# Keys loaded in runs of four positions of a head, and transposed as identity products of single heads on the two column halves

## The chip, the cores and the metric

The kernel runs on one core of one Trainium2 chip. The metric is the device time of one execution in microseconds (us); the time of a kernel is the median of several runs. One further execution is taken with the hardware profiler, and all durations below come from it. PE is the matrix engine (PEld its weight loads), DVE, ACT and POOL are the vector, scalar and GpSimd engines, SP is the engine whose queue issues most DMAs.

## The reference

Attention with a mix of the heads before and after the softmax, then a feed-forward layer with the gate `h - tanh(h)`:

```python
scores = scale * np.matmul(q, k.transpose(0, 1, 3, 2))      # q, k, v: (8, 12, 448, 64)
scores = np.einsum('bhij,hg->bgij', scores, w_pre)          # over the 12 heads
scores = scores - np.max(scores, axis=-1, keepdims=True)
attn = np.exp(scores)
attn = attn / (np.sum(attn, axis=-1, keepdims=True) + 1e-09)
attn = np.einsum('bhij,hg->bgij', attn, w_post)
attn_out = np.matmul(attn, v)
x = attn_out.transpose(0, 2, 1, 3).reshape(3584, 768)
h = x @ w_in                                                # (768, 2048)
out = (h - np.tanh(h)) @ w_out                              # (2048, 768)
```

All data are float32.

## The kernel before, in words

The first half of the program is the attention. Each of the 8 batches is cut into four blocks of at most 120 query positions. For a block the kernel transposes the queries (`prep_q`), multiplies them with the transposed keys (`scores`, tiles `ps_q`, copied to `s`), and lets DMAs regroup the scores so that all 12 heads of 10 positions lie in one tile (`gather`, t<-s, two per place). Then come the mix of the heads (`premix`, tile `ps_p`), the maximum and the exponential (`expo`), the weights of the second mix with the sums of the softmax in them (`norm`, tile `wr`, on POOL), the second mix, which also transposes (`mix`, tile `ps_o`), and the product with the values (`values`, tile `ps_m`, operands `at` and `vr`).

The work is laid out in *places*: one pass of the loop `for p in range(NPL + 3)` (line 1256) handles two groups of 10 positions. A table `todo`, worked out ahead of the loop, says at which place a block's `scores`, `values`, `prep_q`, `prep_k` and loads stand. The order on each engine is the order in which the code is written, and is kept by hand (`in_order`). DMAs on SP are issued in order at the places; the weights of the feed-forward layer are split into parts by `Convert` at the same time (tiles `cr`, `co`, `ct`), with its own loads and stores on the SP queue. The second half of the program is the feed-forward layer.

The keys come in by 24 loads, three for each batch: `load_k(b, hq)` loads four heads. Position `4p + c` of a head goes to partition p (112 partitions, four positions c each). Before, the tile `kr` is laid out as [c, head, d]; a run that is contiguous in memory on both sides is one position of one head, 64 numbers or 256 bytes. `prep_k(b, hp)` then transposes a pair of heads: for each c, the 112x128 numbers of the two heads are one transpose on PE (line 814), which fills 112 columns of a PSUM tile, one head on partitions 0 to 63 and the other on 64 to 127. ACT copies the result as the high part (`kh`, line 825) and DVE subtracts to get the low part (`kl`, line 826). Two `prep_k` calls stand at one place, so the transposes come in groups of eight; there are 24 such groups, of which three belong to the start, ahead of the loop. The values are loaded (`load_v`) as [head, c, d], in runs of four positions or 1 KB.

Of the kernel before, what the change touches and what calls it, by code (L numbers as in the profile page):

```python
# [10 lines left out]
F32 = mybir.dt.float32  # L11
# [10 lines left out]
def raw(ap):  # L22

    return ap.bitcast(F32)
# [126 lines left out]
def kernel_body(  # L151
# [11 lines left out]
    nc = tc.nc  # L163
    B, H, S, D = q.shape
# [4 lines left out]
    CP = 112  # L169
    NC = S // CP  # L170
# [565 lines left out]
    with ExitStack() as st:  # L736

        early, early_ps = ctx.enter_context(ExitStack()), ctx.enter_context(ExitStack())
        ld = early.enter_context(tc.tile_pool(name="ld", bufs=2, side="left"))
# [4 lines left out]
        kp = st.enter_context(tc.tile_pool(name="kp", bufs=1, side="right"))  # L744
# [5 lines left out]
        ident = cst.tile([P, P], F32, name="ident")  # L750
# [3 lines left out]
        kks, vts, krs, qrs, qbs, sts, ats = {}, {}, {}, {}, {}, {}, {}  # L754


        queue, slow, sent = [], [], {}

        def dma(dst, src, to=None):
            entry = [place[0], dst, src, None]  # L760
            (queue if to is None else to).append(entry)
            return lambda places=0: entry[3] is not None and entry[3] + places <= place[0]
# [13 lines left out]

        def load_k(b, hq, t=None):
            if t is None:
                t = ld.tile([CP, NC, 4, D], F32, name="kr", tag="kr", bufs=2)

            sent[b, hq, "k"] = dma(t, k[b, 4 * hq : 4 * hq + 4].rearrange("h (p c) d -> p c h d", c=NC))
            krs[b, hq] = t

        def load_v(b, hq):
# [19 lines left out]
        halves = (slice(0, D), slice(D, P))  # L804

        def prep_k(b, hp, ps=None):


            hq, r = hp // 2, hp % 2
            assert sent[b, hq, "k"]()  # L810
            if ps is None:
                ps = ps_m.tile([P, 512], F32, name="ps_m", tag="ps_m")
            for c in range(NC):
                nc.tensor.transpose(
                    ps[:, c * CP : (c + 1) * CP],
                    krs[b, hq][:, c, 2 * r : 2 * r + 2].rearrange("p j d -> p (j d)"),
                    ident[:CP, :CP],
                )

            def rest():  # L820
                if r == 0:
                    kk = ld.tile([P, 2, 2, S], F32R, name="kk", tag="kk", bufs=KB)
                    kks[b, hq] = kk[:, 0], kk[:, 1]
                kh, kl = kks[b, hq]
                nc.scalar.copy(kh[:, r], ps[:, :S])  # L825
                then.append(lambda: nc.vector.tensor_sub(kl[:, r], ps[:, :S], raw(kh[:, r])))
                if r == 1:
                    del krs[b, hq]

            sooner.append(rest)  # L830
# [79 lines left out]
        def premix(p):  # L910


            pss = [ps_p.tile([P, S], F32, name="ps_p", tag="ps_p") for _ in halves]
            ts = [tg.pop(2 * p + j) for j in range(2)]
            for j in (1, 0):
                for r in (1, 0):
                    k = slice(r * D, D + r * H * half_rows(2 * p + j)[r])
                    nc.tensor.matmul(pss[r][halves[j], :], wpre[k, :], ts[j][k, :], start=True, stop=True)  # L918
            return pss
# [112 lines left out]
        def now(*engines):  # L1032
            place[0] += 1
            engines = engines or (nc.sync,)
            for x in (queue, slow):
                while x:
                    send(x, engines[len(x) % len(engines)])
# [2 lines left out]
        load_q(0)  # L1040
        now()
        for hq in range(3):
            load_k(0, hq, kp.tile([CP, NC, 4, D], F32, name="tmp_k", tag="x", bufs=1) if hq == 2 else None)
        now()
        load_q(1, kp.tile([MT, H, D], F32, name="tmp_q", tag="at", bufs=2))
        now()
# [34 lines left out]
        for w in range(2):  # L1081
            for at in AT[w]:
                x = repeat[:, w, at : at + HP].rearrange("p (i h) -> p i h", i=GH)
# [7 lines left out]
        for w in range(2):  # L1091
            for a in range(2):
                if w == 0:
                    x = both[:, w, a].rearrange("p (i g) -> p i g", i=GH)
                    of, step = ps_w[:, w, :].unsqueeze(1).to_broadcast([P, GH, H]), [[H, GH], [0, H]]
                else:
                    x = both[:, w, a].rearrange("p (g i) -> p g i", i=GH)
# [18 lines left out]
        for r in range(2):  # L1116
            prep_k(0, r, ps_k[:, r])
        flush()
        busy(4, ps_m.tile([P, 512], F32, name="ps_b", tag="ps_m"))
        prep_k(0, 2, bank())  # L1120
        prep_k(0, 3, bank())
        scores_of(0, 0)
        flush()
# [41 lines left out]
        at_s, p, kind = {}, 0, None  # L1165
        window = {i: (lo, hi) for lo, hi, k, i, _ in sorted(halved, reverse=True) if k == "s"}
        while halved:
            ready = sorted((x for x in halved if x[0] <= p), key=lambda x: (x[1], x[3:]))
            if ready:
                x = ready[0]  # L1170
# [3 lines left out]
                if x[2] == kind and other and x[1] > p + 1:  # L1174
                    x = other[0]
# [25 lines left out]
        for i, (b, m) in enumerate(blocks):  # L1201
            p0 = first[i] // 2
            if i + 2 < len(blocks):
                p = at_s[i + 2, 0] - 1
# [7 lines left out]
        for b in range(1, B):  # L1212
            p, o, done = first[blocks.index((b - 1, 1))] // 2 - 4, 0, []
            for hq in range(3):
                if hq == 2:

                    p = max(p, done[0] + 1)
                at_place(p, load_k, b, hq)
                o = max(p + 4, o + 1)
                p += 1  # L1220
                if hq > KB - 4:

                    o = max(o, end_s[blocks.index((b - 1, 3)), hq - 1 - (KB - 4)] + 1)
                for r in range(2):

                    while any(f is prep_q for f, *a in todo[o]) or 2 * len(held(o)) + sum(f is values for f, *a in todo[o]) > 2:
                        o += 1
                    at_place(o, prep_k, b, 2 * hq + r)
                done.append(o)
                assert o < at_s[blocks.index((b, 0)), hq], (b, hq)  # L1230
# [7 lines left out]
        def between0(f):  # L1238
# [10 lines left out]
        start = {  # L1249
            NPL - 3: [partial(load_w0, 0)] + [partial(load_x0, c) for c in range(NK)],  # L1250
            NPL - 2: x0[:1],
            NPL - 1: [partial(load_w0, 1)],
            NPL + 1: [block0.step],
        }
        mixed = None
        for p in range(NPL + 3):
# [13 lines left out]
            if p < NPL:  # L1270
                ps = premix(p)
# [123 lines left out]
```

## Time and profile before

| | |
|---|---|
| time, median of 3 runs | 1708.94 us (1706.41 to 1719.01) |
| the profiled execution's own time | 1703.0 us |
| its span, first to last instruction | 1701.3 us |
| PE busy | 1660.1 us, 98% of the span, 16068 matmul records |
| DVE, ACT, POOL busy | 72%, 64%, 34% |
| mean granted TensorE clock | 0.994 |
| DMA packets under 512 bytes | 105264 of 322290 |

Busy time of PE is counted from a matmul's start to its modelled end, and matmuls overlap; what a matmul costs is therefore read from the distance of one start to the next, not from its duration. Attention and feed-forward layer have different limits, so the rows are read by stage: the places of the attention lie between about 30 and 840 us. Idle time of an engine is put down to what ended it.

### The profile page before, as it was taken

The numbers are of one execution on the slowest core, as the hardware profiler recorded it, in microseconds if no ns is written. First come the engines' busy times: TensorE is split into PE (matmuls) and PEld (weight loads), VectorE is DVE, ScalarE is ACT, GpSimd is POOL, SyncE is SP. The second block draws the span as 40 slices with busy tenths as digits, with TensorE's granted clock in tenths as the row PEclk, the third lists the DMA queues.
The fourth block names the chain that finished last, engine by engine and source line by source line (L and its number), as shares of the span: only waits on it lengthen the run. The fifth ranks groups of instructions, "written<-read, shape, count | busy, mean of one in ns | idle before, by whom it ended". The sixth has DMA issues, their size and how long they took to land.

```text
span 1701.3 us, 41215 instructions
## 1 busy us (share of the span) xinstructions
PE 1660.1 (98%) x16068; PEld 1379.8 (81%) x16068; DVE 1231.3 (72%) x2119; ACT 1091.1 (64%) x1920; POOL 585.5 (34%) x798
## 2 busy tenths in 40 slices
PE   8999999999999899999999999999999999999999
PEld 6777777777777677677788888888888888989999
DVE  5777777878777777675497899868778867778432
ACT  5777777777777677676586777556667456666331
POOL 1466667666666666662100111101001101011100
PEclk9999999999999999999999999999999999999999
DMA  8879889898987979856589899989999989988993
GB/s 183 218 228 257 255 246 276 247 270 259 256 253 231 269 234 257 254 182 208 190 269 340 273 331 318 346 295 335 318 334 362 368 272 327 326 311 327 404 413 132
DMA packets 322290, 475.09 MB, mean 279 GB/s; under 512 B 105264, under 2 KB 255280, under 8 KB 322096
## 3 DMA queue, kind: packets, MB, share of 16 engines
q1 hardware_dynamic: 305660, 414.34, 75.5%
q0 software_dynamic: 16128, 57.68, 8.7%
q8 instruction: 128, 2.10, 0.5%
q14 instruction: 66, 0.54, 0.1%
q10 hardware_dynamic: 308, 0.43, 0.1%
HBM read 274.73 MB, written 120.59 MB: 232 GB/s over the span
## 4 chain that ended last, share of the span: by engine, by line
PE 72%; DMA 7%; DVE 7%; ACT 4%; issue 4%; POOL 4%; SPq 1%; POOLq 0%; ACTq 0%; DVEq 0%
PE ps_o L957 11%; PE ps_h L291 8%; PE ps_h L292 7%; PE ps_h L294 7%; PE ps_m L999 6%; PE ps_p L918 6%; PE y L534 6%; PE y L532 6%; PE y L533 6%; PE ps_q L874 4%; DMA t<-s 2%; DMA gl<-gs 2%; ACT e L929 1%; DVE mx L927 1%; PE y L504 1%
## 5 line engine op out<-in xcount | busy, mean ns | idle before, releaser
L957 PEld LDWEIGHTS ps_o<-wr,e 60*112 60x112 f32 (+1 forms) x5760 | 303.3, 175 | 46.1 <-POOL wr L940 31.9
L957 PE MATMUL ps_o<-wr,e 60*112 60x60 f32 (+1 forms) x5760 | 314.5, 259 | 16.1 <-POOL wr L940 14.6
L929 ACT ACTIVATE e<-ps_p,mx 128x448 f32<-128x448 f32 x360 | 224.8, 631 | 117.2 <-DVE mx L927 82.8
L927 DVE TENSOR_REDUCE mx<-ps_p 128x1 f32<-128x448 f32 x360 | 206.5, 615 | 109.1 <-PE ps_p L918 108.5
L967 ACT COPY at<-ps_o 112x960 f32<-112x960 f32 x156 | 154.3, 989 | 103.4 <-PE ps_o L957 102.9
L918 PE MATMUL ps_p<-t,wpre 60*64 60x448 f32 (+1 forms) x1440 | 182.4, 570 | 6.7 <-DMA t<-s 6.6
L999 PEld LDWEIGHTS ps_m<-at,vr 112*64 112x64 f32 x3072 | 147.6, 137 | 23.0 <-issue 7.7
L999 PE MATMUL ps_m<-at,vr 112*64 112x120 f32 (+1 forms) x3072 | 161.4, 262 | 1.1 <-DMA vr<-in_v_dram 0.9
L532 PE MATMUL y<-w,gh 128*128 128x384 f32 x448 | 151.2, 338 | 2.1 <-DMA w<-wo 1.6
L940 POOL TENSOR_TENSOR wr<-wpost,zs 128x120 f32<-128x120 f32 x180 | 70.0, 389 | 237.6 <-DVE zs L939 199.0
L533 PE MATMUL y<-w,gh 128*128 128x384 f32 x448 | 150.5, 336 | 0.0
L534 PE MATMUL y<-w,gl 128*128 128x384 f32 x424 | 143.4, 338 | 3.0 <-DVE gl L450 3.0
L874 PEld LDWEIGHTS ps_q<-kk,qh 64*120 64x120 f32 (+1 forms) x768 | 59.1, 174 | 82.0 <-issue 45.1
L874 PE MATMUL ps_q<-kk,qh 64*120 64x448 f32 (+1 forms) x768 | 121.8, 394 | 0.9 <-ACT kk L825 0.4
L879 DVE COPY s<-ps_q 120x448 f32<-120x448 f32 (+1 forms) x192 | 112.2, 614 | 9.8 <-PE ps_q L874 8.0
L669 POOL DMA_DIRECT2D gs<-gb x24 | 17.2, 717 | 291.6 <-DVE gb L668 291.6
L307 ACT ACTIVATE u<-h 128x1024 f32<-128x1024 f32 x56 | 59.5, 1063 | 74.4 <-DVE h L716 70.5
L879 ACT COPY s<-ps_q 120x448 f32<-120x448 f32 (+1 forms) x192 | 94.9, 538 | 7.1 <-PE ps_q L874 6.7
L647 POOL DMA_DIRECT2D gs<-ga x24 | 17.2, 716 | 230.0 <-DVE ga L330 222.9
L532 PEld LDWEIGHTS y<-w,gh 128*128 128x128 f32 x448 | 84.2, 188 | 7.2 <-issue 3.5
L533 PEld LDWEIGHTS y<-w,gh 128*128 128x128 f32 x448 | 84.1, 188 | 3.4
L534 PEld LDWEIGHTS y<-w,gl 128*128 128x128 f32 x424 | 79.6, 188 | 4.6 <-DVE gl L450 4.6
(372 smaller groups left out, 3971.3 us busy)
## 6 DMA issues: line engine op xcount, KB each, us to landing
t<-s SPq DMA_DIRECT2D x342, 210.0 KB
wa<-ss SPq DMA_DIRECT2D x96, 384.0 KB
w<-wo SPq DMA_DIRECT2D x43, 768.0 KB
gl<-gs SPq DMA_DIRECT2D x62, 512.0 KB
wa<-wi SPq DMA_DIRECT2D x72, 384.0 KB
w<-ts SPq DMA_DIRECT2D x35, 768.0 KB
gs<-gs POOLq DMA_DIRECT2D x24, 768.0 KB, 9.2
cr<-in_moe_w_in_dram SPq DMA_DIRECT2D x48, 256.0 KB
```

The costliest lines, as they stand in the source:

```text
L291: nc.tensor.matmul(ph, w[:, c, 0], xh, start=start and c == 0, stop=False, skip_group_check=True)
L532: nc.tensor.matmul(y, gh[:, tok], wh, start=first, stop=False, skip_group_check=True)
L533: nc.tensor.matmul(y, gh[:, tok], wl, start=False, stop=False, skip_group_check=True)
L534: nc.tensor.matmul(y, gl[:, tok], wh, start=False, stop=last, skip_group_check=True)
L874: nc.tensor.matmul(ps[:n, :S], qx[a, hp, :], kx[a, hp % 2], start=(x == 0), stop=(x == 2))
L879: eng(sts[i][:n, 2 * hp + j, :], ps[:n, :S])
L918: nc.tensor.matmul(pss[r][halves[j], :], wpre[k, :], ts[j][k, :], start=True, stop=True)
L927: nc.vector.tensor_reduce(out=mx, in_=ps, axis=AX.X, op=ALU.max, negate=True)
L929: nc.scalar.activation(e, ps, AF.Exp, bias=mx, scale=1.0, accum_out=zs[:, 0, r : r + 1])
L957: nc.tensor.matmul(ps[:CP, j, c * GP : (c + 1) * GP].rearrange("p (h i) -> p h i", i=GI)[:, :, r * GH : (r + 1) * GH], e[k, c * CP : (c + ...
L967: nc.scalar.copy(ats[i0][:, :, :, at : at + 2 * GI].rearrange("p c h (j i) -> p j (c h) i", j=2), ps[:CP, :, : NC * GP].rearrange("p j (x ...
L999: nc.tensor.matmul(pv[j * D : (j + 1) * D, r, :n], vt[:, j, c, :], ats[i][:, c, 2 * hp + j, :n], start=(c == 0), stop=(c == NC - 1),)
```

## The change

The tile of a key load is laid out as [head, c, d], like that of the values, so that a contiguous run is four positions of one head (1 KB). With that the two heads of a pair no longer lie side by side for one c, and the transpose of a pair becomes two ordinary matrix products of single heads with the identity matrix: the 112x64 numbers of a head are the stationary operand, the identity is the moving one, and the results go to the lower and the upper half of the partitions of the same PSUM columns (`halves` is the pair of slices 0:64 and 64:128).

```diff
@@ load_k
-                t = ld.tile([CP, NC, 4, D], F32, name="kr", tag="kr", bufs=2)
-
-            sent[b, hq, "k"] = dma(t, k[b, 4 * hq : 4 * hq + 4].rearrange("h (p c) d -> p c h d", c=NC))
+                t = ld.tile([CP, 4, NC, D], F32, name="kr", tag="kr", bufs=2)
+
+            sent[b, hq, "k"] = dma(
+                t.rearrange("p h c d -> p h (c d)"), k[b, 4 * hq : 4 * hq + 4].rearrange("h (p c) d -> p h (c d)", c=NC)
+            )
@@ prep_k
             for c in range(NC):
-                nc.tensor.transpose(
-                    ps[:, c * CP : (c + 1) * CP],
-                    krs[b, hq][:, c, 2 * r : 2 * r + 2].rearrange("p j d -> p (j d)"),
-                    ident[:CP, :CP],
-                )
+                for j, a in enumerate(halves):
+                    nc.tensor.matmul(
+                        ps[a, c * CP : (c + 1) * CP], krs[b, hq][:, 2 * r + j, c], ident[:CP, :CP], start=True, stop=True
+                    )
```

The third load of the first batch, which goes to a tile of its own (`tmp_k`), gets the same layout.

No instruction changes its place. On PE, at the first place of the loop that has a `prep_k`, the order was this (the transposes are L814, between `premix` L918 and `values` L999; the numbers behind the names are output partitions x columns, and x8 is how many follow each other):

```order
L918 MATMUL ps_p<-t,wpre 64x448 x4
L814 MATMUL ps_m<-ident,kr 128x112 x8
L999 MATMUL ps_m<-at,vr 64x120 x24
L957 MATMUL ps_o<-wr,e 112x12x5 x16
L918 MATMUL ps_p<-t,wpre 64x448 x4
```

and is now, with line numbers one higher from the diff on:

```order
L919 MATMUL ps_p<-t,wpre 64x448 x4
L817 MATMUL ps_m<-ident,kr 64x112 x16
L1000 MATMUL ps_m<-at,vr 64x120 x24
L958 MATMUL ps_o<-wr,e 112x12x5 x16
L919 MATMUL ps_p<-t,wpre 64x448 x4
```

Eight transposes of 128 output partitions have become sixteen products of 64, at the same place and between the same neighbours.

On the SP queue, at the first key loads of the loop (between the gathers L907), the order was, with the semaphores that each waits for:

```order
L766 DMA kr<-in_k_dram 112x16x64
L907 DMA t<-s 120x1x448 [waits DVE_49,DMAHW1_49,PE_49,Activation_49]
L907 DMA t<-s 120x1x448 [waits DMAHW2_49]
L766 DMA kr<-in_k_dram 112x16x64
L907 DMA t<-s 120x1x448 [waits DMAHW3_49,PE_49]
```

and is now:

```order
L766 DMA kr<-in_k_dram 112x4x256
L908 DMA t<-s 120x1x448 [waits DVE_49,DMAHW1_49,PE_49,Activation_49]
L908 DMA t<-s 120x1x448 [waits DMAHW2_49]
L766 DMA kr<-in_k_dram 112x4x256
L908 DMA t<-s 120x1x448 [waits DMAHW3_49,PE_49]
```

A load of 112x16 runs of 64 numbers (1792 runs) has become one of 112x4 runs of 256 numbers (448 runs); order and waits are as before.

More of the change, by code (lines that the diff above doesn't have):

```diff
@@ L1042, in kernel_body @@
         for hq in range(3):
-            load_k(0, hq, kp.tile([CP, NC, 4, D], F32, name="tmp_k", tag="x", bufs=1) if hq == 2 else None)
+            load_k(0, hq, kp.tile([CP, 4, NC, D], F32, name="tmp_k", tag="x", bufs=1) if hq == 2 else None)
         now()
```

## The prediction

> **What bounds the kernel now.** I read the page first, then the stretch of the attention in which keys are prepared (30 to 740 us of the span; the last transposes stand at 724): busy time, PE's waits, and the chain that ended last in that stretch.
>
> ```profile
> PE 1660.1 (98%) x16068; PEld 1379.8 (81%) x16068; DVE 1231.3 (72%) x2119; ACT 1091.1 (64%) x1920; POOL 585.5 (34%) x798
> ...
> 30.00:740.00 710.00, 690.38 (x10054) 529.29 (x10050) 528.65 (x1331) 509.87 (x1166) 460.38 (x587) 0.99 0.84 248
> ...
> PE ps_o L957 <- POOL wr L940: 13.4, 16, 1.7
> PE ps_p L918 <- DMA t<-s: 5.0, 7, 1.0
> ...
> by line: PE ps_o L957 20.6%; PE ps_m L999 11.9%; PE ps_p L918 11.8%; issue 7.6%; PE ps_q L874 7.5%; DMA t<-s 4.7%; ACT e L929 3.3%; DVE mx L927 2.2%; PE ps_m L840 1.6%; PE ps_m L814 1.6%; POOL co L103 1.6%; POOL wr L940 1.5%; POOL cm L84 1.
> ```
>
> PE is busy 690 of 710 us there, the next engine (DVE) 529. PE's waits are 13.4 us on `wr` and 5.0 us on gathered scores. PE sets the pace, with stalls in 23 spots. The last row says how much of the transposes is on the chain: 1.6% of 710 is 11.4 us.
>
> **The products.** First, what is one of them? No identity product of single heads is in the trace, but `values` has the same shape: stationary 112x64 out of a tile laid out [head, c, d], float32, results on the two halves of the partitions. It differs in the columns of the moving operand, 120 or 88, between which 112 lies.
>
> ```profile
> L814 PE MATMUL ps_m<-ident,kr x168: 258/259/448, 50.7 to 724.2; 112*128 112x112 f32 x168
> ...
> L814 PE MATMUL ps_m<-ident,kr 112*128 112x112 f32 x168 | 22.2, 279 | 0.0
> ...
> L999 PE MATMUL ps_m<-at,vr 112*64 112x120 f32 x2304 | 128.9, 268 | 1.1 <-DMA vr<-in_v_dram 0.9
> ...
> L999 PE MATMUL ps_m<-at,vr 112*64 112x88 f32 x768 | 32.4, 241 | 0.0
> ```
>
> The durations (279, 268, 241 ns) are near each other and would mislead. The counts say more. The program has 21 groups of 8 transposes in this stretch, 168, and the trace has 168 records: a transpose is one record. `values` is called 64 times with 3 x 4 x 2 = 24 products, 1536, and the trace has 2304 + 768 = 3072: **a float32 product is two records**. What a record costs is read from start to start, in groups (columns: start, length, engine, line, count):
>
> ```profile
> 120.35 2.68 PE L999 MATMUL ps_m<-at,vr 112*64 112x120 f32 x48
> 122.96 1.79 PE L957 MATMUL ps_o<-wr,e 60*112 60x60 f32 x32
> ...
> 129.45 2.04 PE L999 MATMUL ps_m<-at,vr 112*64 112x88 f32 x48
> 131.42 0.80 PE L957 MATMUL ps_o<-wr,e 60*112 60x60 f32 x12
> ...
> 50.72 0.99 PE L814 MATMUL ps_m<-ident,kr 112*128 112x112 f32 x8
> 51.63 2.68 PE L999 MATMUL ps_m<-at,vr 112*64 112x120 f32 x48
> ...
> 203.70 0.98 PE L814 MATMUL ps_m<-ident,kr 112*128 112x112 f32 x8
> 204.62 0.67 PE L874 MATMUL ps_q<-kk,qh 64*120 64x448 f32 x4
> ```
>
> Without its own last record (0.268 and 0.241 us) a group of 48 takes (2.68 - 0.268)/47 = 51.3 ns a record at 120 columns and (2.04 - 0.241)/47 = 38.3 ns at 88; at 112 columns 38.3 + 24/32 x 13.0 = 48.1 ns. Sixteen products are 32 records: 1.54 us. To the next line's start it is 1.97 us (88) and 2.61 us (120) for 48 records, so 2.45 us at 112, of which two thirds are 1.63 us. The transposes take 0.91 to 0.92 us from their start to the next line's. A group gets dearer by 0.71 us by the second way; by the first, with the transposes at (0.98 - 0.259)/7 = 0.103 us, by 1.54 - 8 x 0.103 = 0.72. The longer steps on entering and leaving a group stay as they are, and eight transposes hold a larger share of them, so I add 0.05 and take **0.77 us a group, 24 groups: 18.5 us gross**, bounds 17.0 and 18.7.
>
> The Trainium skill, TensorE: Matmul & The Clock Gate, section Terms, says that the transpose mode of weight loads and matmuls is four times faster for FP32. By that rule an identity product would cost four transposes' time each, a pair of halves running together; the rows of `values` make it a factor of two, and they decide the sum.
>
> **What of it is on the path.** The chain through the stretch meets the transposes here (first and last of 11 pieces, asked for in parts of about 100 us):
>
> ```profile
> 50.79 0.92 PE ps_m L814 x8
> ...
> 722.96 1.69 PE ps_m L814 x8
> ...
> 103.66 1.78 PE L957 MATMUL ps_o<-wr,e 60*112 60x60 f32 x32 [1.56 <-POOL wr L940]
> ...
> 153.33 1.78 PE L957 MATMUL ps_o<-wr,e 60*112 60x60 f32 x32 [0.99 <-POOL wr L940]
> ...
> 210.31 1.78 PE L957 MATMUL ps_o<-wr,e 60*112 60x60 f32 x32 [1.57 <-POOL wr L940]
> ```
>
> Nine pieces of 0.92 and two of about 1.65 make 11.6 us, the 1.6% above. So 11 of the 21 groups delay the end by their full price. The other ten lie ahead of a stall: the groups at 97.1, 146.7 and 203.7 us each have one 6.6 us later, in which PE waits for `wr` behind ACT, DVE and POOL, of 1.56, 0.99 and 1.57 us, longer than 0.77. There the longer group shortens the wait. How much leaks through (ACT must copy these results too) no row shows: between 0 and 10 x 0.77 = 7.7 us; I take a quarter, 1.9, since the three waits seen are all longer than the addition. On the path: 11 x 0.77 + 1.9 = 10.4 us.
>
> The same layout of the array spares something: a group before `values` (the 50.72 row) ends with a step of 0.91 - (0.99 - 0.259) = 0.18 us into the next line, against 0.10 inside. The products have the shape of `values`, so this step should be an ordinary one: 0.08 us, in some six of the groups on the path, **-0.5 us** (0 to -0.9).
>
> **The start.** Three groups stand ahead of the loop, and the chain runs through two of them:
>
> ```profile
> 2.12 8.50 DMA kr<-in_k_dram
> ...
> 10.66 0.99 PE ps_p L814 x8
> ...
> 15.05 0.57 PE ps_p L814 x4
> ...
> 10.66 0.78 PEld L814 LDWEIGHTS ps_p<-ident,kr 112*128 112x128 f32 x8 [0.30 <-DMA kr<-in_k_dram]
> ```
>
> The second load lands at 10.62 us and PE had waited for it 0.30 us only. Faster loads spare those 0.30; behind them is PE itself. The first group, now covered by that landing, comes onto the path. 3 x 0.77 - 0.3 = **+2.0 us** (1.2 to 2.3).
>
> **The loads.** What does a run of 1 KB spare? At the start the queue holds only loads: between 8 and 12 us runs of 256 bytes pass, between 14 and 18 us the values' runs of 1 KB.
>
> ```profile
> 8.00:12.00 4.00, 3.83 (x32) 3.06 (x30) 1.93 (x9) 0.97 (x2) 2.39 (x10) 1.00 1.32 196
> 14.00:18.00 4.00, 3.33 (x28) 2.45 (x26) 2.09 (x4) 1.63 (x4) 0.00 (x0) 1.00 1.12 246
> 138.00:170.00 32.00, 29.16 (x436) 22.96 (x438) 22.26 (x59) 21.77 (x52) 22.57 (x32) 1.00 0.95 263
> ...
> 137.96 0.65 SPq L766 DMA_DIRECT2D kr<-in_k_dram  x1
> ...
> 157.58 0.86 SPq L766 DMA_DIRECT2D kr<-in_k_dram  x1
> 158.61 5.63 SPq L766 DMA_DIRECT2D cr<-in_moe_w_in_dram  x1
> ```
>
> A load of 448 KB takes 459/196 = 2.34 us at the one rate (last column, GB/s) and 1.87 at the other: 0.47 us each, 11 us of transfers in all. Almost all of it lies beside PE's work. It counts where PE waits for gathered scores, 5.0 us in 7 spots around four changes of batch; there the DMA engines are at 0.95 (138 to 170 us), and one key load (137.96) stands at the head of that queue. Half of 0.47 us at four places: **-0.9 us** (0 to -5.0). The load at 157.58 is followed by a DMA that holds SP for 5.63 us; with 448 runs in place of 1792 this hold should shrink, but PE's two waits there were for gathers issued before it, so I count it at nothing.
>
> The Trainium skill, DMA: Bandwidth & Descriptors, section Specifications, says that transfers reach line rate from 512 bytes and that below this a read-modify-write is done. Were the short runs at half rate by that, a load would spare 1.2 us; the trace shows a fifth, 196 against 246 GB/s.
>
> **Sum**, against the profiled execution's 1703.0 us: +10.4 - 0.5 + 2.0 - 0.9 = **+11.0 us**, 1714.0. The median of the runs lies 5.9 us above that execution; on it the forecast is 1708.94 + 11.0 = **1719.9 us**, 0.6% slower. About 1% (17 us) is what a measurement of this kernel can tell from no change.
>
> **Rivals.**
> - *All of it counts.* If the ten covered groups leak fully, because ACT and DVE start on the results as late as PE gives them, it is 18.5 - 0.9 - 0.3 = +17.3: 1726. For it: PE is at 97% in the stretch. Against it: the waits behind these groups. Chance 0.15; half of it lies above 1%.
> - *The stalls soak it up.* The clock falls to half for a few us after long stalls:
>
> ```profile
> core 0: 1701.3 us, clock 0.994
> ...
> 721.00:725.00 4.00, 4.00 (x28) 2.24 (x28) 1.91 (x6) 2.25 (x6) 3.11 (x4) 0.57 1.06 256
> ```
>
>   A clock of 0.994 is 10 us lost over the span, and 0.43 of these 4 us, 1.7, is one such fall. The fall at 721 follows a stall of PE that a group at 700.5 would shorten by 0.77. If two falls vanish (-3.4), the leak is nothing (-1.9) and the gathers come in time (-4.1 more), it is +1.6: 1711. Chance 0.2 for 0 to +6.
> - *Faster than before.* Were a product one record, as a transpose is, 16 records of 48.1 ns would take 0.77 us as eight transposes do, and only the steps, the start and the loads were left: about -2 to -6, 1705. It decides at the record count, which speaks against it: 0.04, and 0.01 that the DMA relief reaches over 1%.
> - *Four times.* If a product takes four transposes' time, a group grows by 8 x 3 x 0.096 = 2.3 us, 24 groups 55 us: 1762. A pair of `values` products at 4 x 0.048 = 0.19 us against a transpose at 0.10 speaks against it. Chance 0.02. This is what the Trainium skill's rule above (TensorE: Matmul & The Clock Gate, Terms) would give.
>
> **Chances and range.** The forecast, +6 to +15, has 0.58; the rivals 0.15, 0.2, 0.05 and 0.02. Slower by over 1% is half of the first rival, the last, and a part of the forecast's upper end with runs that scatter (1706 to 1719 before): 0.18. Faster by over 1%: 0.02. The range, 1708 to 1728, leaves out the fourth rival, most of the third and a few runs beyond.
>
> **What the next profile would show.** L817 (the products) with 24 x 32 = 768 records, near 260 ns each, 1.6 us from the start of a group to the next line, and 0.10 rather than 0.18 us into `values`. PE's wait on `wr` shrinks from 13.4 by 4 to 6 us, above all 6 us behind the groups at 97, 147 and 204. Packets under 512 bytes fall by 24 x 1792 = 43008 to 62256, and no DMA behind a key load holds SP for 5 us. I am wrong if groups of products take 0.9 us, or if PE's stalls stay and the end moves by the whole 18 us.

## The result, and the profile after

| | before | after |
|---|---|---|
| median of 12 runs each, on the same chip (us) | 1707.94 (1702.51 to 1722.94) | 1720.05 (1716.25 to 1727.72) |
| ratio of after to before, 95% interval | | 1.0058 [1.0034, 1.0081] |
| the profiled execution's own time (us) | 1703.0 | 1720.26 |

The kernel is 12.1 us slower by the medians and 9.9 by the ratio; by the interval, 5.8 to 13.8 us. The forecast was 1719.9. The spans of the two profiled executions lie 17.2 us apart, since that of before is one of its quickest. Here and below, an execution that is far slower than the others of its kernel, at a lower granted clock, is left out of times and ratios.

The page of after, with the rows that answer to the first ones of the prediction and the packets:

```profile
span 1718.5 us, 42367 instructions
PE 1677.4 (98%) x16644; PEld 1398.6 (81%) x16644; DVE 1233.7 (72%) x2119; ACT 1093.1 (64%) x1920; POOL 585.8 (34%) x798
...
DMA packets 290038, 475.16 MB, mean 276 GB/s; under 512 B 62256, under 2 KB 223024, under 8 KB 289840
```

PE has 576 records more: 24 groups of 32 instead of 8. The short packets fell by 43008, exactly the runs of the 24 key loads. The products by themselves (columns: count, ns least/median/most, first and last start):

```profile
L817 PE MATMUL ps_m<-ident,kr x672: 259/259/447, 52.6 to 742.4; 112*64 112x112 f32 x168
...
L817 PE MATMUL ps_k<-ident,kr x32: 259/259/310, 8.6 to 10.1; 112*64 112x112 f32 x32
```

21 x 32 = 672 records in the loop, 32 in each group of the start. The record is 259 ns long, as that of a transpose was: the length tells nothing of the price. The timeline of PE does:

```profile
52.59 1.75 PE L817 MATMUL ps_m<-ident,kr 112*64 112x112 f32 x32
54.17 2.63 PE L1000 MATMUL ps_m<-at,vr 112*64 112x120 f32 x48
...
100.15 1.75 PE L817 MATMUL ps_m<-ident,kr 112*64 112x112 f32 x32
101.83 0.67 PE L875 MATMUL ps_q<-kk,qh 64*120 64x448 f32 x4
...
106.95 1.78 PE L958 MATMUL ps_o<-wr,e 60*112 60x60 f32 x32 [1.01 <-POOL wr L941]
...
156.63 1.78 PE L958 MATMUL ps_o<-wr,e 60*112 60x60 f32 x32 [0.22 <-POOL wr L941]
158.72 0.98 PE L919 MATMUL ps_p<-t,wpre 60*64 60x448 f32 x8 [0.30 <-DMA t<-s]
...
170.76 0.98 PE L919 MATMUL ps_p<-t,wpre 60*64 60x448 f32 x8 [1.76 <-DMA t<-s]
...
217.30 1.79 PE L958 MATMUL ps_o<-wr,e 60*112 60x60 f32 x32 [1.01 <-POOL wr L941]
```

A record costs (1.75 - 0.259)/31 = 48.1 ns from start to start. From the group's start to the next line it is 1.58 us ahead of `values` and 1.68 ahead of `scores`, where the transposes took 0.91 and 0.92. The stalls behind the groups at 97, 147 and 204 us of before are shorter, 1.01, 0.22 and 1.01 us against 1.56, 0.99 and 1.57. But a gather is waited for longer than any was in that profile of before, 1.76 us at 170.76 (a second profile of before, below, has one of 1.7). PE's waits in the stretch from 30 to 740 us:

```profile
PE ps_o L958 <- POOL wr L941: 10.8, 16, 1.7
PE ps_p L919 <- DMA t<-s: 5.9, 5, 2.3
PE ps_p L919 <- ACT at L968: 1.2, 1, 1.2
```

### The profile page after: what moved, and what is told of

Read it like the earlier page. It is cut to its first block, busy times and chain, and to the rows that moved or that the text cites. A ratio compares the mean times of both kernels' runs of the same rounds, so it can differ in the third digit from the quotient of the medians.

```text
span 1718.5 us, 42367 instructions
## 1 busy us (share of the span) xinstructions
PE 1677.4 (98%) x16644; PEld 1398.6 (81%) x16644; DVE 1233.7 (72%) x2119; ACT 1093.1 (64%) x1920; POOL 585.8 (34%) x798
## 4 chain that ended last, share of the span: by engine, by line
PE 74%; DMA 10%; DVE 5%; ACT 4%; issue 3%; POOL 3%; SPq 1%; POOLq 0%; ACTq 0%; DVEq 0%
PE ps_o L958 11%; PE ps_h L291 7%; PE ps_h L294 7%; PE ps_p L919 7%; PE ps_h L292 7%; PE ps_m L1000 7%; PE y L532 6%; PE y L534 6%; PE y L533 6%; PE ps_q L875 5%; DMA t<-s 3%; PE ps_m L817 2%; DMA gl<-gs 1%; DMA wo<-co 1%; DMA ts<-ct 1%
## 5 line engine op out<-in xcount | busy, mean ns | idle before, releaser
L1000 PEld LDWEIGHTS ps_m<-at,vr 112*64 112x64 f32 x3072 | 149.2, 138 | 22.2 <-ACT at L975 7.3
L669 POOL DMA_DIRECT2D gs<-gb x24 | 17.2, 717 | 291.4 <-DVE gb L668 291.4
L647 POOL DMA_DIRECT2D gs<-ga x24 | 17.2, 716 | 230.1 <-DVE ga L330 223.0
```

The costliest lines, as they stand in the source:

```text
L1000: nc.tensor.matmul(pv[j * D : (j + 1) * D, r, :n], vt[:, j, c, :], ats[i][:, c, 2 * hp + j, :n], start=(c == 0), stop=(c == NC - 1),)
```

## The experiments

All ratios are to the kernel before, run on the same chip beside them.

### The loads alone, twice, and the kernel before once more

The 1-KB runs go into the old tile; the transposes stay.

```diff
+                t.rearrange("p c h d -> p (c h d)").rearrange("p (h x) -> p h x", h=4),
+                k[b, 4 * hq : 4 * hq + 4].rearrange("h (p c) d -> p h (c d)", c=NC),
```

> The keys are loaded in runs of 1 KB into the tile as it was before, and the transposes stay; the numbers land permuted, so the result is another one, while every instruction and its size is that of before but for the loads. Theory P (the products alone cost the time; the loads are worth nearly nothing): within 0.2% of before, 0 to -2 us, of which 0.3 at the start; the transposes keep 0.92 us a group. Rival L (the loads change what queues up at a change of batch, and a part of the 12 us is theirs): 3 to 6 us slower, with longer waits of PE for gathered scores. Rival H (the loads help and hide a larger price of the products): 3 to 5 us faster. In all three the packets under 512 bytes are 62256, and no DMA behind a key load holds SP for 5 us.

> The loads alone (runs of 1 KB, transposes as before) once more, for a second profile; the heads and positions of the keys come out mixed. If long waits at the changes of batch belong to the new loads, it has again more falls of the clock than the kernel before (eleven in the first profile, against six) and waits for gathered scores above 6 us; if they are scatter, it may have six or fewer, and a span within 3 us of 1701.

> The kernel before once more, for a second profile. It tells how far the waits for gathered scores and the falls of the clock differ from one execution to the next without any change. If the 0.8 to 7 us that the loads alone seemed to cost are scatter, this profile has other falls of the clock than the first (six) and other waits for gathered scores than 5.0 us, by 2 us or more; if they belong to the loads, it has the same six within one, and 5.0 us within 1.

Measured: 1710.88 us, ratio 1.0024 [1.0005, 1.0044], so the loads cost 0.9 to 7.5 us where they were to spare some; Rival L came nearest. The mean granted clock of these runs is 0.9895, against 0.9915 in the runs of before beside them, and that alone is 3.4 us of 1708. In the two profiles of this kernel the clock falls to half 10 and 10 times (the eleven of the second expectation count one that begins 0.6 us before the end), for 3.4 or 6.8 us each, and 24.2 and 22.2 us are lost by it (the span times what the clock lacks to 1). The two profiles of before have 6 and 5 such falls and lose 10.4 and 13.7 us. PE waits 6.4 and 6.0 us for gathered scores between 30 and 740 us, against 5.0 and 4.8. The windows from 170 to 180 us (columns: us; busy time of PE, PEld, DVE, ACT, POOL; granted clock; DMA share; GB/s), of the second profile of before, then of the first and the second of the loads alone:

```profile
170.00:180.00 10.00, 10.00 (x150) 7.37 (x144) 5.77 (x17) 6.03 (x16) 4.76 (x8) 1.00 0.91 293
```

```profile
170.00:180.00 10.00, 10.00 (x104) 7.48 (x106) 3.61 (x11) 2.85 (x8) 1.73 (x5) 0.67 0.81 267
```

```profile
170.00:180.00 10.00, 9.81 (x126) 7.19 (x128) 4.93 (x13) 4.01 (x10) 2.59 (x6) 0.83 0.86 277
```

The clock is 1.00 in the first and 0.67 and 0.83 with the new loads. What stands ahead of it is a wait for a gather of the new batch; again before, loads alone (first, second):

```profile
165.09 0.98 PE L918 MATMUL ps_p<-t,wpre 60*64 60x448 f32 x8 [0.80 <-DMA t<-s]
169.79 0.98 PE L918 MATMUL ps_p<-t,wpre 60*64 60x448 f32 x8 [0.78 <-DMA t<-s]
```

```profile
169.93 1.77 PE L921 MATMUL ps_p<-t,wpre 60*64 60x448 f32 x8 [1.97 <-DMA t<-s]
```

```profile
170.19 1.77 PE L921 MATMUL ps_p<-t,wpre 60*64 60x448 f32 x8 [1.49 <-DMA t<-s]
```

Two waits of 0.8 us leave the clock alone. One of 1.5 to 2.0 us is followed by a premix of 1.77 us instead of 0.98, at half the clock. On SP the order of the issues is the same, but the hold behind the key load is gone. After:

```profile
163.95 0.94 SPq L766 DMA_DIRECT2D kr<-in_k_dram  x1
165.07 1.41 SPq L766 DMA_DIRECT2D cr<-in_moe_w_in_dram  x2
```

Before, the load at 157.58 us was followed by an issue that held SP for 5.63 us (3.45 in the second profile); now the weights' two loads follow in 1.41 us (1.43 and 1.13 with the loads alone), ahead of the next gathers. Gathers issued at 165 to 171 us then land after 8.0 to 9.5 us in the two profiles of the loads alone, after 5.9 to 7.1 us in the first of before, and under 5.6 us in the second. That the missing hold is what crowds these gathers, and that this costs the time, is an argument from order and time; no run isolates it. The run with long query runs, further below, speaks against it: there no hold over 3 us is left, the gathers of 159 to 173 us take 8.1 to 9.2 us to land, and yet PE waits for gathers only 2.2 us. The second profile of before also limits it: its own time is 1711.39 us, 8.4 more than the first with nothing changed, 6.1 of them lost by 216 us. Single long waits are scatter; what repeats is the time lost to the clock. Why these loads should cost clock stays open.

### The products alone

The old loads and tile, with products of single heads.

```diff
-                nc.tensor.transpose(
-                    ps[:, c * CP : (c + 1) * CP],
-                    krs[b, hq][:, c, 2 * r : 2 * r + 2].rearrange("p j d -> p (j d)"),
+                for j, a in enumerate(halves):
+                    nc.tensor.matmul(
+                        ps[a, c * CP : (c + 1) * CP], krs[b, hq][:, c, 2 * r + j], ident[:CP, :CP], start=True, stop=True
```

> The keys are loaded as before, in runs of 256 bytes, and transposed by the sixteen products of single heads. Theory P: as the changed kernel, ratio 1.005 to 1.008 (9 to 14 us), start a little later than there since the second load lands late (0.3 us). Rival L: 1.002 to 1.004. Rival H: 1.009 or more. The holds of 5 us behind the third key load of a batch should be back if they hang on 1792 short runs.

Measured: 1721.03 us (five runs), ratio 1.009 [1.006, 1.0121]. That is just above Theory P and at the mark of Rival H, and the interval reaches both. The groups stand exactly as in after, and the holds of 4.5 to 5.5 us behind the third key loads are back, so the holds hang on the loads and not on the products. The products carry the whole cost and no part of the loads is needed for it. The intervals of this run and of the whole change (1.0058) overlap, so they do not rank the two; the middles of the two parts, 1.009 and 1.0024, add up to more than the whole, while their lower ends, 1.006 and 1.0005, fit into its interval. What the new loads do where the products are in place is therefore not measured.

### The products twice

Every product of after issued twice into the same place.

> The changed kernel with each product done twice, 64 records a group in place of 32. A group should take 3.2 us to the next line. If a stall covers a group only up to its own length, the stalls are used up by now and nearly all of 24 x 1.54 = 37 us counts: 30 to 36 us over the changed kernel, 42 to 48 over before (ratio 1.025 to 1.028). Rival: a fixed quarter leaks through at the ten covered groups: 14 x 1.54 + 10 x 0.39 = 25 us over the changed kernel, 37 over before (1.022).

Measured: 1748.34 us, ratio 1.0235 [1.0213, 1.0258]. This lies between the two forecasts, 1.025 and 1.022, and the interval reaches both; the timeline has to tell them apart. Behind the group that stood at 97 us:

```profile
108.48 3.29 PE L818 MATMUL ps_m<-ident,kr 112*64 112x112 f32 x64
111.70 0.67 PE L876 MATMUL ps_q<-kk,qh 64*120 64x448 f32 x4
...
116.83 1.78 PE L959 MATMUL ps_o<-wr,e 60*112 60x60 f32 x32 [1.01 <-POOL wr L942]
118.55 1.77 PE L920 MATMUL ps_p<-t,wpre 60*64 60x448 f32 x8
```

The group is 1.54 us longer than in after, and the stall behind it is still **1.01 us, as in after**. The stall had hidden 0.55 us of the first addition and hides none of the second. The queue of DVE, the vector engine, says why. Here are its copy of the scores, its subtraction for `kl`, and the last step of `zs`, which POOL needs for `wr`: before, after, and in this kernel.

```profile
98.92 0.62 DVE L879 COPY s<-ps_q 120x448 f32<-120x448 f32 x1 [0.57 <-PE ps_q L874]
100.01 1.16 DVE L826 TENSOR_TENSOR kk<-ps_m,kk 128x448 fp32r<-128x448 f32 x2 [0.46 <-ACT kk L825]
102.91 0.17 DVE L939 RECIPROCAL zs<-zs 128x2 f32<-128x2 f32 x1
```

```profile
102.76 0.62 DVE L880 COPY s<-ps_q 120x448 f32<-120x448 f32 x1 [1.32 <-PE ps_q L875]
103.31 1.15 DVE L827 TENSOR_TENSOR kk<-ps_m,kk 128x448 fp32r<-128x448 f32 x2
106.20 0.17 DVE L940 RECIPROCAL zs<-zs 128x2 f32<-128x2 f32 x1
```

```profile
112.64 0.62 DVE L881 COPY s<-ps_q 120x448 f32<-120x448 f32 x1 [2.86 <-PE ps_q L876]
113.18 1.15 DVE L828 TENSOR_TENSOR kk<-ps_m,kk 128x448 fp32r<-128x448 f32 x2
116.08 0.17 DVE L941 RECIPROCAL zs<-zs 128x2 f32<-128x2 f32 x1
```

On DVE, `zs` stands behind the subtraction, and the subtraction behind the copy of the scores, which PE makes after the group. Counted from the start of the group (97.06 us before), this copy begins after 1.86, 2.61 and 4.16 us: it carries each addition in full. Before, DVE then waited for ACT's copy of the transposes, and the subtraction began 1.09 us after the copy of the scores; after, ACT is done in time, DVE waits no more, and it is 0.55 us. These 0.54 us of waiting were the slack. The first addition uses them up, `zs` comes 0.20 us later (6.05 for 5.85), and the second addition passes whole (7.60). The stall beyond moves along instead of shrinking.

### Five covered groups alone

The old kernel, with products only for the five key loads whose groups stand at 97, 147, 204, 352 and 558 us, each ahead of a stall.

```diff
+                if (b, hq) in ((1, 2), (2, 0), (2, 2), (4, 0), (6, 0)):
```

> Before, with products in only five of the 24 groups, those at 97, 147, 204, 352 and 558 us that a stall of PE for wr follows 6.6 us later. If the stalls cover them: each of the five sets PE back by 0.77 us at first and by 0.2 to 0.5 after the next L957, 1 to 2 us in all, ratio 1.000 to 1.001. Rival (the price counts wherever it falls): 5 x 0.77 = 3.9 us, 1.0023. The profile should tell this better than the times.

Measured: 1709.29 us, ratio 0.9994 [0.998, 1.0009]. The full price, 1.0023, lies outside, but the mean clock of these runs is 0.994, against 0.9915 beside them, which is worth 4 us; so the times alone do not decide. The timeline does; the same stall, once more:

```profile
97.60 1.75 PE L816 MATMUL ps_m<-ident,kr 112*64 112x112 f32 x32
...
104.41 1.78 PE L963 MATMUL ps_o<-wr,e 60*112 60x60 f32 x32 [1.01 <-POOL wr L946]
```

0.76 us in, 0.55 out: 0.21 us leaks at this group, as in after, with nothing else changed.

### What makes a product dear: its records

The products of after on the upper two bytes of each number, single heads on the two halves.

```diff
+                        ps[a, c * CP : (c + 1) * CP], krs[b, hq][:, 2 * r + j, c].bitcast(mybir.dt.bfloat16)[:, 1::2], identb[:CP, :CP], start=True, stop=True
```

> As the changed kernel, but each product takes only the upper two bytes of each key number (a 2-byte stationary operand and a 2-byte identity); the keys are cut to that. Theory: the price of a group is that a float32 product is two records. With 2-byte operands a product should be one record, sixteen a group (384 in all), and a group falls from 1.6 us to the next line to between 0.8 and 1.0 us, about what eight transposes took; the set-back of 0.76 us a group goes and the time is back near the kernel before: 1706 to 1711 us, ratio 0.999 to 1.002. Rival: what costs is that there are sixteen instructions on half of the columns instead of eight; then a group stays above 1.3 us, and the time at 1716 to 1721, ratio 1.004 or more.

And the old kernel, with one float32 product of a pair of heads in place of each transpose, on all columns.

> The kernel before, with each transpose of a pair replaced by one float32 product of the pair with the identity, on all 128 columns: eight instructions a group, sixteen records expected. Theory: the two halves of a pair of single heads run side by side, so that a full-width record takes twice the 48 ns from start to start, and the price is float32's second record alone: a group takes 1.5 to 1.7 us to the next line, ratio 1.005 to 1.010, as with the single heads. Rival: a record costs 48 ns whatever its width, and the change pays for sixteen instructions in place of eight: a group takes 0.8 to 1.0 us, as the transposes, ratio 0.998 to 1.002.

Measured: 1710.54 us, ratio 1.0013 [0.999, 1.0036], and 1732.23 us, ratio 1.0122 [1.0085, 1.0159]. The group in each, first the two-byte products, then the full-width ones:

```profile
50.83 0.58 PE L819 MATMUL ps_m<-identb,kr 112*64 112x112 bf16 x16
51.24 2.64 PE L1002 MATMUL ps_m<-at,vr 112*64 112x120 f32 x48
```

```profile
53.09 2.04 PE L814 MATMUL ps_m<-ident,kr 112*128 112x112 f32 x16
55.06 1.15 PE L1001 MATMUL ps_m<-at,vr 112*64 112x120 f32 x18
```

Sixteen two-byte instructions are sixteen records and take 0.41 us to the next line: (0.58 - 0.213)/15 = 24.5 ns each, where a float32 product is 2 x 48.1 = 96.2 ns. So not the number of instructions is dear, but float32: two records, each of twice the price. The two-byte group is half as long as was expected; that the time fell into its range all the same is luck, for what the group spared went into PE's waits for `wr` (17.4 us for 13.4) and into the clock (0.988 on the mean of the runs, 0.991 beside them). On all columns a record takes (2.04 - 0.275)/15 = 118 ns and the group 1.97 us, longer than the 1.5 to 1.7 expected and worse than the change: a float32 record on all columns costs more than twice one on half of them. Two single heads side by side (4 x 48.1 = 192 ns) are cheaper than a pair in one product (2 x 117.7 = 235), and both are dearer than a transpose (103).

### Cheaper than a transpose

The old kernel with one two-byte product of a pair in place of each transpose.

```diff
+                    krs[b, hq][:, c, 2 * r : 2 * r + 2].rearrange("p j d -> p (j d)").bitcast(mybir.dt.bfloat16)[:, 1::2],
+                    identb[:CP, :CP],
```

> The kernel before (loads in runs of 256 bytes), with each transpose of a pair of heads replaced by one product with the identity of the upper two bytes of both heads' numbers: eight instructions of 128 output partitions a group, the keys cut to 2 bytes. With one record each at the 26 ns that sixteen records of the half size took, or at twice that, a group should take 0.2 to 0.5 us to the next line instead of 0.92. Theory: what a shorter group spares is worth its full price where no stall follows, in 11 groups of the loop and at the start, 14 x 0.4 to 0.7 us, and little in the ten ahead of a stall: 5.5 to 10 us, 1698 to 1703 us, ratio 0.994 to 0.997, faster than both kernels. Rival: the stalls take it back (in the run with 2-byte products of single heads PE's wait for the second mix's weights was 17.4 us instead of 13.4, and the time did not fall): ratio 0.998 to 1.002.

Measured: 1710.56 us, ratio 0.9991 [0.9969, 1.0013]: no gain, though each group takes 0.42 us less (a record (0.57 - 0.213)/7 = 51 ns). The timeline of PE and its waits from 30 to 740 us:

```profile
50.68 0.57 PE L816 MATMUL ps_m<-identb,kr 112*128 112x112 bf16 x8
51.17 2.68 PE L1003 MATMUL ps_m<-at,vr 112*64 112x120 f32 x48
...
103.17 2.54 PE L961 MATMUL ps_o<-wr,e 60*112 60x60 f32 x32 [2.05 <-POOL wr L944]
105.64 1.77 PE L922 MATMUL ps_p<-t,wpre 60*64 60x448 f32 x8
```

```profile
PE ps_o L961 <- POOL wr L944: 17.9, 20, 2.0
```

The stall behind the group at 97 us grows from 1.56 to 2.05 us, and now the clock falls behind it: mix and premix take 2.54 and 1.77 us instead of 1.78 and 0.98. PE's waits for `wr` are 17.9 us instead of 13.4, and the mean clock of the runs is 0.988 against 0.990, some 4 us. The rival's account came true: a shorter group hands its time to the stalls, and longer stalls can cost clock. No kernel tried here is faster than the one before.

### The queries in runs of 3 KB

After, with query loads contiguous over 12 x 64 numbers.

```diff
+            flat = q[b].rearrange("h s d -> (h s) d").rearrange("(s h) d -> s (h d)", h=H)
```

> As the changed kernel, but the queries are loaded in contiguous runs of 3 KB instead of 256 bytes; the numbers come in another order. Theory: the holds of SP for 3 to 6 us stand behind loads of over a thousand short runs, whichever tensor they load; with the key loads in runs of 1 KB only the query loads are left to cause them, so none over 3 us should remain in the attention, and the sum of holds over 0.9 us falls from 69 us to 30 to 50. Packets under 512 bytes fall from 62256 by 43008 to about 19248. If PE's waits for gathered scores around the changes of batch come from these loads, they fall from 5.9 us by 2 to 4 and the time by as much: 1713 to 1718. Rival, that the gathers themselves fill the DMA engines and short runs of loads do not matter: holds go or stay, the waits stay at 4 to 7 us and the time at that of the changed kernel within 2 us.

Measured: 1717.75 us, ratio 1.005 [1.0027, 1.0072], not separable from after's 1.0058. The holds went as expected: none over 3 us is left, and what they last beyond 0.9 us falls from 69 to 36 us in sum. So did the waits, from 5.9 us:

```profile
PE ps_p L922 <- DMA t<-s: 2.2, 4, 0.7
```

So the holds do stand behind loads of over a thousand short runs, whichever tensor they load (a query load has 12 x 120 runs of 256 bytes). What their removal is worth in time lies within the scatter of the runs.

## Why the prediction held, point by point

- **The price of a group** held. Forecast 0.77 us, bounds 0.71 to 0.78; measured 0.76 ahead of `scores` and 0.67 ahead of `values`, from 32 records of 48.1 ns. Counting records and interpolating between two rows of `values` gave it, and the run with two-byte products shows that float32 is the reason. The Trainium skill, FP8 and Floating Point Precision, section TensorE Precision Notes, says that true FP32 goes through the array in four passes; the runs agree, 96.2 against 24.5 ns on half of the columns (3.9) and 235 against 51 on all (4.6). The Trainium skill's rule in TensorE: Matmul & The Clock Gate, section Terms, that transpose mode is four times faster for FP32, does not agree: 235/103 = 2.3, and 192/103 = 1.9 for a pair of halves. The sum of that rival is a little off as well: with the transpose's own 0.103 us a group grows by 2.5 us, 59 in all, and 1708.94 + 59 is 1768, not 1762.
- **The step into `values`** was foreseen, but too small and for too few groups. It was to fall from 0.18 to 0.10 us, 0.08 us in some six groups. It did (0.67 us to the next line ahead of `values`, 0.76 ahead of `scores`), and the first records of `values` gain 0.05 us more: each such group sets the next place back by 0.62 us. Eight of the eleven on the chain stand ahead of `values`. Read place by place (the start of each premix, after against before), the eleven cost 8 x 0.62 + 2.1 for the three ahead of `scores` = 7.0 us; the prediction had 11 x 0.77 - 0.5 = 8.0.
- **The covered groups**: the term was too small and its reason wrong. A quarter of 7.7 us, 1.9, was to leak, because the stalls are longer than the addition. Three of the ten (77, 671 and 700 us) are ahead of `values` and cost their 0.62 in full; the other seven, ahead of `scores`, leave 0.20 to 0.50 us each: 1.9 + 2.4 = 4.3 us. The length of the stall does not decide it: behind doubled products 1.01 us of stall remain and the whole second addition goes through. What can be hidden is the slack on the way from the group to `wr`, DVE's wait for ACT's copy: 0.25 to 0.69 us at the seven groups before, of which they hid 0.26 to 0.56, at none more than its slack (to 0.02 us). The prediction looked at the stall at the end of that way. The chain of after, in the same parts, shows it too; it meets 16 of the 21 groups instead of 11, such as these, which were covered before:

```profile
100.22 1.68 PE ps_m L817 x32
...
210.56 1.68 PE ps_m L817 x32
...
571.14 1.68 PE ps_m L817 x32
```

- **The start** held: +1.86 us for +2.0. The rows of after:

```profile
11.37 1.75 PE L817 MATMUL ps_p<-ident,kr 112*64 112x112 f32 x32
...
16.30 1.75 PE L817 MATMUL ps_p<-ident,tmp_k 112*64 112x112 f32 x32 [0.67 <-issue]
```

No key load is waited for any more, as foreseen: PE comes to the second load's group at 11.37 us, later than that load landed before (10.62).
- **The loads** did not do what was forecast. -0.9 us was half of the time spared by longer runs, at four changes of batch. The rate rose less than assumed (196 to 215 GB/s from 8 to 12 us, not 246), the gathers' median time to land did not move (5.2 and 5.1 us), and beside the old transposes the new loads cost 0.9 to 7.5 us, most of it together with a lower clock. The failed step is "half of 0.47 us at four places": it took the time of transfers for what PE's waits depend on. What they do depend on is open; beside the products, the sign of the term is not measured.
- **What the profile was to show**: records, steps and packets came out so. No hold follows a key load, but holds of 3.4 to 4.8 us now stand behind query loads. PE's wait for `wr` shrank by 2.6 us and not 4 to 6, for the reason given at the covered groups.
- **The sum**: 7.0 + 4.3 + 1.9 = 13.2 us by the places, where the prediction's terms made 11.9 without the loads and 11.0 with them. The medians give 12.1 and cannot tell these apart. At the end of the attention the profile of after lies 19.0 us behind that of before; the other 5.8 us arise at the changes of batch, where the second profile of before loses too, 6.9 us by the same place. That the total came so near is in part luck: the groups on the chain were priced 1.0 us too high, the covered ones 2.4 too low, and the loads were counted as a gain. Rival one (all counts, 17.3 us) fell with the interval and with the stall behind the five covered groups; rival two (stalls soak it up) with the doubled products, and no fall of the clock vanished (six in both profiles, 10.4 and 10.5 us lost); "faster" and "four times" fell with the records and their distance.

## What to carry to other kernels

Price a matrix product by its records and their distance from start to start, and look whether float32 doubles both; a record's length says nothing. What a stall behind a step can hide is not the stall's length but the slack on the way from the step to what the stall waits for: follow that way through the queues of the other engines, and look where one of them idled for something else. A gain that only lengthens a stall can be lost to the clock, so read the granted clock beside every wait, and beside every ratio.

## What the runs showed of the hardware

- Two float32 products on the two halves of the columns cost 192 ns from start to start, one product on all of them 235 ns. That the two run side by side is the likely reading; no row shows one of them alone.
- A stall of 1 to 2 us can halve the clock for 3.4 us (1.49 us with the loads alone, 1.01 us with doubled products) or for 6.8 us (2.05 us with two-byte pairs, 1.97 us with the loads alone), and need not: 1.56 us before did not, and of the two stalls of 1.01 us in after, the one at 217.30 did (clock 0.51 from 219.5 to 222.9 us) and the one at 106.95 did not (1.00). What decides is open. In every profile the falls begin whole multiples of 3.41 us apart. The Trainium skill, TensorE: Matmul & The Clock Gate, section What's actually happening, puts the fall after an idle window of about 3.4 us; that length is seen here as the step of the slow stretches, while the stalls ahead were shorter.
- The mean clock of the runs moved with the change: 0.988 with the two kernels whose groups are shorter (0.990 and 0.991 beside them), 0.994 with the doubled products and with the five covered groups (0.9915 beside them). A thousandth of it is 1.7 us here.
- The third key load of a batch, 1792 short runs, kept SP from its next DMA for 3.5 to 6.1 us in six of the batches in the two profiles of before; some query loads of 1440 short runs did so for 3.4 to 4.8 us after. Key loads of 448 runs of 1 KB did not.
